# Seven block products in place of eight in two of four dense layers, and a contraction-outer loop in the other two

## The chip, the cores and the metric

The program runs on one core of one Trainium2 chip. The time is device microseconds of one execution; lower is better. A profiled execution gives the trace from which all rows below are read.

## The reference, cut to what matters

Two batches of 448 tokens, 12 heads of width 64, give 768 channels. The attention has a soft cap (tanh) ahead of the softmax. Its output goes through an RMS norm and two feed-forward blocks, all in float32:

```python
scores = cap * np.tanh(scale * (q @ k.T) / cap)          # 2 x 12 heads, 448 x 448
attn = softmax(scores); x = attn @ v                      # 896 tokens x 768
xn = x / rms(x) * rms_g
y = (silu(xn @ w_gate) * (xn @ w_val)) @ w_out            # 768 -> 2 x 1536 -> 768
h = y @ w_in; g = max(h, 0) + alpha * min(h, 0)           # 768 -> 2048
out = g @ w_out2                                          # 2048 -> 768
```

## The kernel before

**Products in three parts.** TensorE multiplies in a 32-bit format of reduced precision (`F32R`). Every float32 operand is therefore split into a rounded part and the rest (`h` and `l`, "hi" and "lo"), and a product takes three matmuls: `wh*xh`, `wh*xl`, `wl*xh`. A matmul here has a 128x128 weight tile and 448 moving columns (one batch of tokens, a "half"). `products` writes them: for each of `n_k` contraction tiles, three matmuls for each half.

**Weights.** All weights lie in one stream of 68 units of six 128x128 tiles in 64-bit floats. A unit is loaded (`w_load`, 768 KB), turned into a 32-bit float by a ScalarE cast (`w_abs`) and a VectorE operation (`w_bits`, line 96), and split by ScalarE (`w_hi`) and VectorE (`w_lo`, line 113). `step(u)` does this some units ahead, once per unit that TensorE has used up.

**Layers.** An output tile of 128 channels is made at a time, with all its contraction tiles in one PSUM bank for each half. The layer gate/value takes 24 output tiles of 6 contraction tiles, `w_out` 6 of 12, `w_in` 16 of 6 and the last 6 of 16: 864 + 432 + 576 + 576 = 2448 matmuls.

**Attention.** 48 steps (12 pairs of heads, four groups `g`): `qk`, then the ScalarE functions in `soft`, then `pv` of two steps before. Hooks put with `at(n, ...)` follow step `n`: `prep` (VectorE splits q and k of the next pair), `evac` (the PSUM results `oa`, `ob` are copied to SBUF, and a row of sums goes by DMA to `gt`), `recip` (VectorE reciprocal of the row sums of two pairs, then two GpSimd-issued DMAs that put them in `r2`, called r in the trace), `norm` (TensorE spreads `r2` over partitions into `rps`, VectorE multiplies, and squares are summed for the RMS), `rms` and `xnorm`. GpSimd computes only the squares and their sums.

**The passage from attention to the layers.** The last pairs' `recip`, `norm` and `rms` run beside `fill(m, 0)`: five half-size products that need only the first batch. Then `xnorm_last` makes the second batch's operand, `fill(m, 1)` uses it, and the main loop begins.

**Order.** Each engine runs its instructions in the order in which the program writes them (`manual_schedule`). TensorE, VectorE, ScalarE and GpSimd each have one queue; DMAs are issued from SP's queue, apart from those of `recip` and one constant (GpSimd's) and another constant (ScalarE's).

Of the kernel before, what the change touches and what calls it, by code (L numbers as in the profile page):

```python
# [17 lines left out]
P = 128  # L18
# [20 lines left out]
NFILL = 2  # L39
# [6 lines left out]
def attn_moe_kernel(ctx: ExitStack, tc: tile.TileContext, qk_in, v, sel, w, gvec, alpha, cap, out):  # L46
# [4 lines left out]
    hfill = ctx.enter_context(tc.tile_pool(name="hfill", bufs=1))  # L51
    tmp = ctx.enter_context(tc.tile_pool(name="tmp", bufs=2))
# [34 lines left out]
    def w_abs(u):
        if u < n_units and u not in top_t:
            top_t[u] = tops[u % 2]
            nc.scalar.copy(top_t[u].bitcast(F16)[:, 1::2], raw_t[u].bitcast(BF16)[:, 4:4 * UW + 4:4])  # L90

    def w_bits(u, parts=(0, 1)):
        if u < n_units and 1 in parts and u not in bits_t:
            t = wpool.tile([P, UW], U32, tag="wt", name="wt", bufs=3)
            bits_t[u] = t
            nc.vector.scalar_tensor_tensor(  # L96
                out=t, in0=raw_t[u].bitcast(U32)[:, 1:2 * UW + 1:2], scalar=13, in1=top_t[u],
                op0=ALU.logical_shift_right, op1=ALU.bitwise_or,
            )

    def w_hi(u, home=None):
        if u < n_units and u not in wh_t:
            if home is None:
                wh_t[u] = wpool.tile([P, UK, P], F32R, tag="wh", name="wh", bufs=4)
            else:
                wh_t[u], wl_t[u] = home()
            nc.scalar.copy(wh_t[u], bits_t[u].bitcast(F32).rearrange("p (k m) -> p k m", m=P))  # L107

    def w_lo(u, force=False):
        if u < n_units and (force or u not in wl_t):  # L110
            if not force:
                wl_t[u] = wpool.tile([P, UK, P], F32R, tag="wl", name="wl", bufs=4)
            nc.vector.tensor_tensor(  # L113
                out=wl_t[u], in0=bits_t[u].bitcast(F32).rearrange("p (k m) -> p k m", m=P), in1=wh_t[u],
                op=ALU.subtract,
            )
# [79 lines left out]
    ea, eb, xt, gt = {}, {}, {}, {}  # L196
# [40 lines left out]
    def norm(i):  # L237
# [3 lines left out]
        x = sb.tile([P, S], F32, tag="xt", name="xt", bufs=6)  # L241
        xt[i] = x
# [18 lines left out]
    def rms(b):  # L261
# [3 lines left out]
        rstd[b] = sb.tile([P, S], F32, tag="rstd", name="rstd", bufs=1)  # L265
# [3 lines left out]
    xh, xl = {}, {}  # L269

    def xnorm(i):
        b, p = divmod(i, NP)
        if p == 0:
            xh[b] = xpool.tile([P, KD, S], F32R, tag=f"xh{b}", name="xh")
            xl[b] = xpool.tile([P, KD, S], F32R, tag=f"xl{b}", name="xl")
        xn = sb.tile([P, S], F32, tag="xn", name="xn", bufs=1)
        nc.vector.scalar_tensor_tensor(
            out=xn, in0=xt.pop(i), scalar=g_t[:, p:p + 1], in1=rstd[b], op0=ALU.mult, op1=ALU.mult
        )
        nc.vector.tensor_copy(xh[b][:, p, :], xn)  # L280
# [20 lines left out]
    def products(dst, j0, n_k, rh, rl, halves, tail=None):


        for kx in range(n_k):
            u, o = divmod(j0 + kx, UK)
            first, last = kx == 0, kx == n_k - 1
            for hs in halves:
                nc.tensor.matmul(dst(hs), wh_t[u][:, o, :], rh(kx, hs), start=first, stop=False)  # L308
            for hs in halves:
                nc.tensor.matmul(dst(hs), wh_t[u][:, o, :], rl(kx, hs), start=False, stop=False)  # L310
            for hs in halves:
                nc.tensor.matmul(dst(hs), wl_t[u][:, o, :], rh(kx, hs), start=False, stop=last)  # L312
            if tail and o == UK - 1:
                tail(u)

    hh, hl = {}, {}
    xhf = lambda kx, hs: xh[hs][:, kx, :]
    xlf = lambda kx, hs: xl[hs][:, kx, :]

    def gate_a(sg, gp):  # L320
        nc.scalar.activation(out=sg, in_=gp, func=AF.Sigmoid)
        nc.vector.tensor_tensor(out=sg, in0=gp, in1=sg, op=ALU.mult)

    def gate_b(f, sg, vp, hsl):
        nc.vector.tensor_tensor(out=sg, in0=vp, in1=sg, op=ALU.mult)
        nc.scalar.copy(hh[f][:, hsl], sg)
        yield
        nc.vector.tensor_tensor(out=hl[f][:, hsl], in0=sg, in1=hh[f][:, hsl], op=ALU.subtract)

    def h_tiles(pool, f):  # L330
        hh[f] = pool.tile([P, 2, S], F32R, tag=f"hh{f}", name="hh")
        hl[f] = pool.tile([P, 2, S], F32R, tag=f"hl{f}", name="hl")

    def run(gen):
        for _ in gen:
            pass

    fill_ps, fill_t, sgs = {}, [None], {}

    def fill(n, half):  # L340

        f, which = divmod(n, 2)
        if half == 0 and which == 0 and f < NFILL:
            h_tiles(hfill, f)
# [307 lines left out]
```

## Time and profile before

| | |
|---|---|
| time, median of 3 runs | 630.99 us (630.76 to 631.55) |
| time of the profiled execution | 632.72 us |
| its span, first to last instruction | 630.7 us |
| TensorE busy | 617.6 us, 98% |
| VectorE busy | 299.3 us, 47% |
| ScalarE busy | 308.4 us, 49% |
| GpSimd busy | 34.3 us, 5% |
| mean granted TensorE clock | 0.997 of full |

The shares are means over the whole span. Matmuls are pipelined, so that a busy TensorE is not one at its peak: the pitch from one matmul's start to the next one's says more. The share of the other engines says little on its own, since each stage has its own mix; what ends each wait is in the rows below.

### The profile page before, as it was taken

The numbers are of one execution on the slowest core, as the hardware profiler recorded it, in microseconds if no ns is written. First come the engines' busy times: TensorE is split into PE (matmuls) and PEld (weight loads), VectorE is DVE, ScalarE is ACT, GpSimd is POOL, SyncE is SP. The second block draws the span as 40 slices with busy tenths as digits, with TensorE's granted clock in tenths as the row PEclk, the third lists the DMA queues.
The fourth block names the chain that finished last, engine by engine and source line by source line (L and its number), as shares of the span: only waits on it lengthen the run. The fifth ranks groups of instructions, "written<-read, shape, count | busy, mean of one in ns | idle before, by whom it ended". The sixth has DMA issues, their size and how long they took to land.

```text
span 630.7 us, 6973 instructions
## 1 busy us (share of the span) xinstructions
PE 617.6 (98%) x2852; PEld 538.0 (85%) x2852; DVE 299.3 (47%) x356; ACT 308.4 (49%) x368; POOL 34.3 (5%) x33
## 2 busy tenths in 40 slices
PE   5999989999999999999999999999999999999997
PEld 4666656678999999999999999999999999999996
DVE  7349766958645554444443331455555552232200
ACT  5899979934443443333332223566665652322300
POOL 0013521320000000000000000000000000000000
PEclk9999989999999999999999999999999999999999
DMA  7476464130143333322343331332333224243200
GB/s 244 158 257 223 147 221 139 29 103 0 51 150 101 101 105 125 121 101 101 106 144 120 123 109 50 101 101 100 104 122 123 103 87 150 111 162 130 79 30 29
DMA packets 19039, 73.47 MB, mean 116 GB/s; under 512 B 6080, under 2 KB 6464, under 8 KB 19008
## 3 DMA queue, kind: packets, MB, share of 16 engines
q1 hardware_dynamic: 15456, 72.81, 33.2%
q0 software_dynamic: 3408, 0.23, 0.5%
q8 instruction: 22, 0.36, 0.2%
q14 instruction: 9, 0.07, 0.0%
q10 hardware_dynamic: 144, 0.00, 0.0%
HBM read 70.14 MB, written 2.75 MB: 116 GB/s over the span
## 4 chain that ended last, share of the span: by engine, by line
PE 86%; ACT 7%; DMA 3%; DVE 2%; issue 1%; POOL 0%; DVEq 0%; POOLq 0%; ACTq 0%
PE m L308 24%; PE m L310 24%; PE m L312 24%; PE s L162 4%; PE oa L188 3%; ACT pt L173 3%; PE ob L192 2%; ACT pt L172 2%; DMA r<-tl 2%; PE fs L308 1%; PE fs L310 1%; PE fs L312 1%; DMA rw<-qk_in 1%; ACT top L90 1%; DMA gt<-eb 1%
## 5 line engine op out<-in xcount | busy, mean ns | idle before, releaser
L113 DVE TENSOR_TENSOR wl<-wt,wh 128x768 fp32r<-128x768 f32 x67 | 64.2, 958 | 105.6 <-ACT wh L107 105.5
L90 ACT CAST top<-raw 128x768 f16<-128x768 bf16 x68 | 73.0, 1073 | 29.5 <-DMA raw<-w_in 29.5
L107 ACT CAST wh<-wt 128x768 fp32r<-128x768 f32 x67 | 55.5, 828 | 35.9 <-DVE wt L96 19.9
L96 DVE SCALAR_TENSOR_TENSOR wt<-raw,top 128x768 uint32<-128x768 uint32 x68 | 64.6, 951 | 1.6 <-ACT top L90 1.6
L308 PE MATMUL m<-xh,wh 128*128 128x448 f32 x228 | 64.8, 365 | 0.0
L312 PE MATMUL m<-xh,wl 128*128 128x448 f32 x228 | 64.7, 365 | 0.0
L310 PE MATMUL m<-xl,wh 128*128 128x448 f32 x228 | 64.7, 365 | 0.0
L312 PE MATMUL m<-zh,wl 128*128 128x448 f32 x192 | 57.1, 365 | 0.0
L310 PE MATMUL m<-zl,wh 128*128 128x448 f32 x192 | 57.1, 365 | 0.0
L308 PE MATMUL m<-zh,wh 128*128 128x448 f32 x192 | 57.1, 365 | 0.0
L162 PE MATMUL s<-hi 128*128 128x448 f32 x96 | 49.7, 517 | 6.5 <-DVE hi L387 6.5
L310 PE MATMUL m<-y_xl,wh 128*128 128x448 f32 x192 | 54.5, 365 | 0.0
L308 PE MATMUL m<-y_xh,wh 128*128 128x448 f32 x192 | 54.5, 365 | 0.0
L312 PE MATMUL m<-y_xh,wl 128*128 128x448 f32 x192 | 54.5, 365 | 0.0
L172 ACT ACTIVATE pt<-s,cinv 128x896 f32<-128x896 f32 (+1 forms) x48 | 43.5, 907 | 6.7 <-PE s L162 5.2
L173 ACT ACTIVATE pt<-pt,cap_t 128x896 f32<-128x896 f32 (+1 forms) x48 | 45.6, 950 | 1.6
L310 PEld LDWEIGHTS m<-xl,wh 128*128 128x128 f32 x228 | 42.8, 188 | 3.4
L308 PEld LDWEIGHTS m<-xh,wh 128*128 128x128 f32 x228 | 42.8, 188 | 3.4
L312 PEld LDWEIGHTS m<-xh,wl 128*128 128x128 f32 x228 | 42.8, 188 | 3.4
L192 PE MATMUL ob<-pt,vt 128*128 128x448 f32 x96 | 42.0, 543 | 0.0
L310 PE MATMUL m<-hl,wh 128*128 128x448 f32 x144 | 40.9, 365 | 0.0
L308 PE MATMUL m<-hh,wh 128*128 128x448 f32 x144 | 40.9, 365 | 0.0
(122 smaller groups left out, 927.2 us busy)
## 6 DMA issues: line engine op xcount, KB each, us to landing
raw<-w_in SPq DMA_DIRECT2D x68, 768.0 KB, 4.3
rw<-qk_in SPq DMA_DIRECT2D x11, 928.0 KB, 4.9
vt<-v_in SPq DMA_DIRECT2D x12, 416.0 KB, 5.5
out<-o SPq DMA_DIRECT2D x5, 448.0 KB, 2.7
rw<-qk_in SPq DMA_DIRECT2D x1, 480.0 KB, 4.4
rw<-qk_in SPq DMA_DIRECT2D x1, 448.0 KB, 5.5
out<-o SPq DMA_DIRECT2D x2, 224.0 KB, 1.9
gt<-ea SPq DMA_DIRECT2D x12, 1.8 KB, 1.6
```

What stands on the lines that cost most here:

```text
L90: nc.scalar.copy(top_t[u].bitcast(F16)[:, 1::2], raw_t[u].bitcast(BF16)[:, 4:4 * UW + 4:4])
L96: nc.vector.scalar_tensor_tensor(out=t, in0=raw_t[u].bitcast(U32)[:, 1:2 * UW + 1:2], scalar=13, in1=top_t[u], op0=ALU.logical_shift_right ...
L107: nc.scalar.copy(wh_t[u], bits_t[u].bitcast(F32).rearrange("p (k m) -> p k m", m=P))
L113: nc.vector.tensor_tensor(out=wl_t[u], in0=bits_t[u].bitcast(F32).rearrange("p (k m) -> p k m", m=P), in1=wh_t[u], op=ALU.subtract,)
L162: nc.tensor.matmul(s[:, n, :S], hi[i][:, S + o:S + o + P], t[hd], start=(m == 0), stop=(m == len(mm) - 1),)
L172: nc.scalar.activation(out=t[:, :n], in_=s[:, :n, :S], func=AF.Tanh, scale=cinv)
L173: nc.scalar.activation(out=t[:, :n], in_=t[:, :n], func=AF.Exp, scale=cap_t)
L188: nc.tensor.matmul(oa[i][:, :S], lhs, r, start=(h == "A" and c == 0), stop=(h == "T"))
L192: nc.tensor.matmul(ob[i][:, :S], lhs, r, start=(h == "T"), stop=(h == "B" and c == 2))
L308: nc.tensor.matmul(dst(hs), wh_t[u][:, o, :], rh(kx, hs), start=first, stop=False)
L310: nc.tensor.matmul(dst(hs), wh_t[u][:, o, :], rl(kx, hs), start=False, stop=False)
L312: nc.tensor.matmul(dst(hs), wl_t[u][:, o, :], rh(kx, hs), start=False, stop=last)
```

## The change

The layers with 768 inputs (gate/value, called `g`, and `w_in`, called `z`) are cut into 2x2 blocks: the weight in output halves and contraction halves (`A11` to `A22`), the input in contraction halves and batches (`B11` to `B22`). Seven block products take the place of eight. They need sums of weight blocks (`S1` to `S4`, made on GpSimd from the 32-bit weights), differences of input blocks (`T1` to `T4`, VectorE), and sums of the products (`u2`, `u3`, `add22`, `add21`, `add12`, on VectorE; a first copy on ScalarE). Each sum and difference is split into hi and lo again.

A "slot" is one product of one unit: 18 matmuls for one group `g` of output tiles. There are 6 groups in layer `g` and 4 in layer `z`; the first two groups go side by side, the others one after another. All other work hangs on slots as hooks: `do(n, rank, fn)` puts `fn` behind the matmuls of slot `n` in program order. The four weight blocks of a group are converted by `conv` (cast and bits).

The layers `w_out` (`o`) and the last (`f`) have the contraction outside and three output tiles at a time; a slot is one unit of 36 matmuls. Their inputs are split by `ksplit`.

In the attention phase the copy of `ob` (`eb`) moves from ScalarE to VectorE, eight units are converted in place of seven, and the eight weight sums of the first two groups are made there. The diff, cut to its core:

```diff
+    def w_sum(out, a, b, op, home=None):
+        t = f_t[home] if home else f_tile()
+        nc.gpsimd.tensor_tensor(out=t, in0=f_t[a], in1=f_t[b], op=op)
+        f_t[out] = t
...
+    def sums(lay, g):
+        n = (lay, g)
+        w_sum((*n, "S1"), (*n, "A21"), (*n, "A22"), ALU.add)
+        w_sum((*n, "S3"), (*n, "A11"), (*n, "A21"), ALU.subtract, home=(*n, "A21"))
...
-            nc.scalar.copy(eb[i], ob.pop(i)[:, :S])
+            nc.vector.tensor_copy(eb[i], ob.pop(i)[:, :S])
...
+    def product(ps, u, name, first):
+        wh, wl = h_t.pop(u), l_t.pop(u)
+        xh, xl = oper[name]
+        for r in range(2):
+            mm = [(a[:, r * K3 + k, :], x[:, k, :]) for k in range(K3) for a, x in ((wh, xh), (wh, xl), (wl, xh))]
+            for n, (lhs, rhs) in enumerate(mm):
+                nc.tensor.matmul(
+                    ps[:, r, :S], lhs, rhs, start=first and n == 0, stop=n == len(mm) - 1,
...
+        for u in conv_seq[:2]:
+            at(3, w_load, u)
+        for j, u in enumerate(conv_seq[:]):
+            s0 = 7 + 5 * j
+            at(s0, w_top, u)
+            at(s0 + 1, w_bits, u)
+            if j < 6:
+                at(s0 + 1, w_next, u)
+            if u[2] in ("A11", "A12"):
+                at(s0 + 2, w_hi, u)
+                at(s0 + 3, w_lo, u)
+            if u[2] == "A22":
+                at(s0 + 2, sums, "g", u[1])
+                at(s0 + 3, sum2, "g", u[1])
+            if u[2] == "A12":
+                at(s0 + 4, sum4, "g", u[1])
...
         recip(len(members) - 1)
-        fill(0, 0)
+        product(pa[0], ("g", 0, "A11"), "B11", True)
         norm(last - 3)
         norm(last - 2)
-        fill(1, 0)
+        first_sum(0, ct("c21"))
+        product(pa[1], ("g", 1, "A11"), "B11", True)
         norm(last - 1)
         norm(last)
-        fill(2, 0)
+        first_sum(1, ct("c21"))
+        product(pa[0], ("g", 0, "A12"), "B21", False)
+        w_hi(("g", 0, "S1"))
         rms(B - 1)
...
+        product(pa[1], ("g", 1, "A12"), "B21", False)
+        w_lo(("g", 0, "S1"))
+        w_hi(("g", 1, "S1"))
+        for i in range((B - 1) * NP, (B - 1) * NP + K3):
+            xnorm(i)
...
+        def operand(name, src):
+            pool = xpool if name in ("B11", "B21", "B22") else main
+            h, l = (pool.tile([P, K3, S], F32R, tag=f"{name}{p}", name=f"x{p}") for p in "hl")
+            nc.scalar.copy(h, src)
+            tt(l, src, h, ALU.subtract)
+            oper[name] = (h, l)
+
+        def t1(b11, b12):
+            tt(b11, b12, b11, ALU.subtract)
+            operand("T1", b11)
...
+        t1(x0[:, lo3], x1[:, lo3])
+        for i in range((B - 1) * NP + K3, B * NP):
+            xnorm(i)
+        w_lo(("g", 1, "S1"))
...
+        STEADY = ("P1", "P6", "P5", "P7", "P2", "P4", "P3")
...
+        layer("g", G1, ("P5", "P6", "P7", "P4", "P3"))
...
+        layer("z", G2, ("P1", "P5", "P2", "P6", "P7", "P4", "P3"))
...
+            if n >= 2:
+                early = u[2] == "A11" and u[1] >= 2
+                do(n - 2 - early, 0, w_hi, u)
+                do(n - 2 - early, 2, w_lo, u)
...
+                for d, x in ((-6, "A11"), (-5, "A21"), (-4, "A22"), (-2, "A12")):
+                    convs.append((b + d, (lay, g, x)))
+                do(b - 4, 4, sums, lay, g)
+                do(b - 3, 4, sum2, lay, g)
+                do(b + 3, 4, sum4, lay, g)
...
+            do(at_["P6"] + 1, 1, u2_first if both else u2, g, lambda: cu("c12"))
+            do(at_["P7"] + 1, 1, u3, g, lambda: cu("c22"))
+            do(at_["P7"] + 1, 1, add22, g)
+            do(at_["P7"] + 2, 1, gate, g, 3, c22, None)
+            do(at_["P4"] + 1, 1, add21, g)
+            do(at_["P4"] + 2, 1, gate, g, 2, c21, None)
+            do(at_["P3"] + 1, 1, add12, g)
+            do(at_["P3"] + 2, 1, gate, g, 1, c12, None)
+        do(0, 0, t2, x0[:, lo3], x1[:, hi3])
+        do(1, 5, t3, x1[:, lo3], x1[:, hi3])
+        do(3, 5, t4, x0[:, hi3], x0[:, lo3])
+        do(5, 5, operand, "B22", x1[:, hi3])
...
+        do(z0, 1, lambda: operand("B21", yf[1][:, lo3]))
+        do(z0 + 2, 1, lambda: t2(yf[0][:, lo3], yf[1][:, hi3]))
+        do(z0 + 4, 5, lambda: t3(yf[0][:, hi3], yf[1][:, hi3]))
+        do(z0 + 6, 5, lambda: t4(yf[1][:, lo3], yf[0][:, lo3]))
+        do(z0 + 8, 5, lambda: operand("B22", yf[1][:, hi3]))
...
+        f0 = at_of["f", 0, 0]
+        do(f0 - 2, 5, ksplit, "f", 0, zt, ("T2h", "T2l", "T1h"), ("B11h", "B11l", "kx"))
```

## Rows read from the trace of the kernel before

**Rows 1.** Waits of TensorE: line waited for, total us, times, longest us.

```profile
PE rps L240 <- DMA r<-tl: 2.8, 2, 2.1
PE fo L310 <- DVE xl L296: 0.2, 1, 0.2
```

**Rows 2.** Timeline of TensorE: start us, us, instruction; ends are modelled, starts count.

```profile
126.36 0.71 PE L308 MATMUL fs<-xh,wh 128*128 128x448 f32 x1
...
146.00 0.37 PE L308 MATMUL fo<-xh,w_fill 128*128 128x448 f32 x1
...
148.47 0.36 PE L308 MATMUL fo<-xh,wh 128*128 128x448 f32 x1
...
339.99 0.57 PE L308 MATMUL m<-hh,wh 128*128 128x448 f32 x2
...
342.42 0.56 PE L308 MATMUL m<-hh,wh 128*128 128x448 f32 x2
```

**Rows 3.** Instruction groups by line and shape: busy us, mean ns, idle before.

```profile
L113 DVE TENSOR_TENSOR wl<-wt,wh 128x768 fp32r<-128x768 f32 x67 | 64.2, 958 | 105.6 <-ACT wh L107 105.5
L96 DVE SCALAR_TENSOR_TENSOR wt<-raw,top 128x768 uint32<-128x768 uint32 x68 | 64.6, 951 | 1.6 <-ACT top L90 1.6
...
L328 DVE TENSOR_TENSOR hl<-sg,hh 128x896 fp32r<-128x896 f32 x10 | 10.9, 1092 | 2.4 <-ACT hh L326 1.2 <-issue 0.2
...
L325 DVE TENSOR_TENSOR sg<-m,sg 128x896 f32<-128x896 f32 x10 | 10.9, 1091 | 24.6 <-PE m L312 24.6
...
L326 ACT CAST hh<-sg 128x896 fp32r<-128x896 f32 x10 | 9.5, 947 | 43.9 <-DVE sg L325 41.8 <-issue 2.1
...
L291 DVE SCALAR_TENSOR_TENSOR xn_last<-xt,g_t,rstd 128x448 f32<-128x448 f32 x6 | 4.0, 680 | 0.0
...
L328 DVE TENSOR_TENSOR hl<-sgf,hh 128x448 fp32r<-128x448 f32 x4 | 2.5, 625 | 2.5 <-ACT hh L326 2.5
```

**Rows 4.** Timeline of VectorE, late in the attention phase.

```profile
104.48 2.95 DVE L267 RECIPROCAL rstd<-rstd 128x448 f32<-128x448 f32 x1 [4.18 <-ACT rstd L266]
...
128.19 0.63 DVE L281 TENSOR_TENSOR xl<-xn,xh 128x448 fp32r<-128x448 f32 x1
```

**Rows 5.** Timeline at the end of attention, SP's queue, TensorE and VectorE; last, landing of r's DMAs.

```profile
127.47 0.50 SPq L206 DMA_DIRECT2D gt<-eb  x1
...
135.35 0.65 PE L240 MATMUL rps<-r,sel_t 128*128 128x448 f32 x2 [0.72 <-DMA r<-tl]
...
144.91 1.28 DVE L291 SCALAR_TENSOR_TENSOR xn_last<-xt,g_t,rstd 128x448 f32<-128x448 f32 x2
...
DMA to landing us min/median/max: 2.0/4.2/8.3
```

**Rows 6.** Timeline of VectorE and GpSimd where both work, and where they don't collide.

```profile
117.71 0.96 DVE L96 SCALAR_TENSOR_TENSOR wt<-raw,top 128x768 uint32<-128x768 uint32 x1
117.82 1.64 POOL L251 TENSOR_TENSOR sq<-xt 128x448 f32<-128x448 f32 x1 [5.33 <-DVE xt L244]
...
118.59 1.35 DVE L277 SCALAR_TENSOR_TENSOR xn<-xt,g_t,rstd 128x448 f32<-128x448 f32 x1
...
119.54 1.41 POOL L255 TENSOR_TENSOR s<-s,sq 128x448 f32<-128x448 f32 x1
...
119.98 1.23 DVE L280 CAST xh<-xn 128x448 fp32r<-128x448 f32 x1
...
123.41 0.39 DVE L280 CAST xh<-xn 128x448 fp32r<-128x448 f32 x1
...
137.85 0.62 DVE L244 TENSOR_TENSOR xt<-eb,rps 64x448 f32<-64x448 f32 x1
137.93 1.15 POOL L255 TENSOR_TENSOR s<-s,sq 128x448 f32<-128x448 f32 x1 [2.12 <-ACT sq L253]
```

**Rows 7.** Stretches of TensorE: length, busy us, granted clock, DMA share, GB/s.

```profile
83.60:85.70 2.10, 0.00 (x0) 1.00 0.53 193
85.70:89.20 3.50, 3.49 (x10) 0.51 0.46 141
```

More of the change, by code (lines that the diff above doesn't have):

```diff
@@ L87, in w_abs @@
[L87 to L116, printed above, removed]
+        raw_t[u] = wpool.tile([P, 4 * UW + 4], U16, tag="raw", name="raw", bufs=2)
@@ L194, in pv @@
             del q2[i], hi[i], vt[i]
-    ea, eb, xt, gt = {}, {}, {}, {}
+    ea, eb, gt = {}, {}, {}
+    xf = [xpool.tile([P, KD, S], F32, tag=f"b{b + 1}", name="xf") for b in range(B)]
     group = {}
@@ L301, in products @@
[L301 to L344, printed above, removed]
-        if (f, half) not in ((NFILL, 0), (0, 1)):
-            if which == 0:
-                fill_t[0] = ps_s.tile([P, 2, 512], F32, tag="s", name="fs")
-            t = fill_t[0][:, which, :S]
-        else:
-            t = ps_o.tile([P, 512], F32, tag="o", name="fo")[:, :S]
-        fill_ps[f, half] = fill_ps.get((f, half), ()) + (t,)
-        products(lambda hs: t, n * UK, KD, xhf, xlf, [half])
@@ L571, in attn_moe_kernel @@
[L571 to L588 removed]
+            return pair_tile(*pools[(turn[0] - 1) % 4])
@@ new lines, in attn_moe_kernel, with layer @@
+        STEADY = ("P1", "P6", "P5", "P7", "P2", "P4", "P3")
+        def layer(lay, n_g, start):
+            for p in start:
+                for g in range(2):
+                    pslot(lay, p, g)
+            for g in range(2, n_g):
+                for p in STEADY:
+                    pslot(lay, p, g)
+        hb, zt = {}, {}
+        layer("g", G1, ("P5", "P6", "P7", "P4", "P3"))
+        for half in range(2):
+            for u in range(K1 // 2):
+                oslot("o", half, u, K1 // 2, lambda kk, l: 2 * kk + l)
@@ new lines, in attn_moe_kernel, with h_of @@
+        for g in range(2):
+            do(z0 - 2, 4, sums, "z", g)
+            do(z0 - 1 + g, 4, sum2, "z", g)
+            do(z0 + 3 + g, 4, sum4, "z", g)
+        convs.sort(key=lambda c: c[0])
+        for n, u in convs:
+            conv_seq.append(u)
+            do(n, 3, conv, u)
+        for u in conv_seq[6:8]:
+            do(0, 6, w_next, u)
+        def h_of(g):
+            if g % 2 == 0 and g // 2 not in hb:
+                hb[g // 2] = block(g // 2)
+            return hb[g // 2][:, g % 2 * 4:g % 2 * 4 + 4, :]
@@ new lines, in attn_moe_kernel, with u2_first @@
+        twelve = {}
+        def u2_first(g, _):
+            if g == 0:
+                twelve[0] = block(3)
+            u2(g, lambda: twelve[0][:, 2 * g:2 * g + 2, :])
+        for g in range(G1):
+            at_ = {p: at_of.get(("g", g, p)) for p in STEADY}
+            both = g < 2
+            if not both:
+                do(at_["P1"] + 1, 1, lambda g: first_sum(g, ct("c21")), g)
+            do(at_["P2"] + 1 if not both else g, 1, gate, g, 0, pa, (lambda: cu("c11")) if both else (lambda: ct("c11")))
+            do(at_["P6"] + 1, 1, u2_first if both else u2, g, lambda: cu("c12"))
[6 more added lines that the diff above has]
+            do(at_["P3"] + 2, 1, gate, g, 1, c12, None)
@@ new lines, in attn_moe_kernel, with y_put @@
+        o0 = at_of["o", 0, 0]
+        do(o0 - 2, 5, ksplit, "o", 0, hb, ("T2h", "T2l", "T3h"), 3)
+        do(o0 - 1, 5, ksplit, "o", 1, hb, ("T3l", "B21h", "B21l"), 0)
+        do(o0 + 2, 5, ksplit, "o", 2, hb, ("T4h", "T4l", "B22h"), 1)
+        yf = {}
+        def y_put(half):
+            yf[half] = block(2 + half)
+            for m in range(3):
+                nc.scalar.copy(yf[half][:, m:m + 4:3, :], banks[m][:, :, :S])
+        y0 = at_of["o", 1, 0]
+        do(y0 - 1, 9, y_put, 0)
+        do(y0 + 1, 5, lambda: operand("B11", yf[0][:, lo3]))
```

399 lines of the change are left out of this document (239 added, 160 removed).

## The prediction

> **What bounds the kernel now.** I read first the waits of TensorE: behind its start it waits 3.0 us in all, for the row sums at the end of a pair of heads and for one split [rows 1]. Then the timeline of its matmuls. In the main loop twelve starts take 342.42 - 339.99 = 2.43 us, 0.2025 us for each, without a gap [rows 2]. The five half-size fills run from 126.36 to 148.47 us: 22.1 us for 90 matmuls worth 18.2, so that the whole passage from attention into the layers costs 3.9 us [rows 2]. TensorE bounds everything behind 126 us, and VectorE's 47% hides there. A matmul less is therefore worth 0.2025 us, as long as the other queues keep up.
>
> **What is removed.** Each group of output tiles takes seven slots of 18 matmuls in place of eight, with ten groups: 180 matmuls fewer, 2268 for 2448. That is 180 x 0.2025 = **-36.5 us**. A slot lasts 18 x 0.2025 = 3.65 us. The product's order (nine matmuls in a row into one bank, one half) is that of the fills; from 146.00 to 148.47 us those took 0.206 a matmul [rows 2]. On the 1260 matmuls of the new slots that is 0 to 4.2 us; the timeline has no slot of the new kind in the main pools, and I take half, **+2.1**.
>
> **Prices.** VectorE: a split or bit operation of 768 columns 0.96 and 0.95 us, an operation of 896 columns 1.09 whether its input lies in PSUM or SBUF, of 448 columns 0.62, the normalization 0.68 [rows 3]. The step from 448 to 896 gives 1.56 for the 1344 columns of an input block. ScalarE: 0.95 for 896, in proportion 0.81 for 768 and 1.42 for 1344. A difference T takes VectorE, then a ScalarE copy that VectorE's queue waits for, then VectorE: 1.56 + 1.42 + 1.56 = 4.55. Each VectorE operation starts some 0.03 us behind the last.
>
> GpSimd's weight sums are not in the trace. A sum of 448 columns takes 1.15 us [rows 6], in proportion 1.97 for 768; there are 40. What do they cost VectorE? From 117.71 to 121.21 us three VectorE operations that alone take 0.95, 0.68 and 0.39 [rows 3, 6] needed 3.50 us beside two GpSimd operations: 1.48 us lost, 0.74 for each, 1.27 in proportion for 768. VectorE's multiplication from PSUM at 137.85 took its usual 0.62 beside a sum [rows 6]. About a third of VectorE's work in the layers reads PSUM (6.1 of the 18.5 us of a group, below), so a sum costs VectorE between 0 and 1.97 us; I take **0.9** there and 1.27 in the attention phase, nearest the collision seen.
>
> [...]
>
> **The start.** VectorE works without a pause from 104.48 to 128.82 us [rows 4], since the reciprocal stands in its queue until ScalarE delivers. Before, that delayed nobody: ScalarE evacuated the last `ob`, and its DMA left at 127.47 [rows 5]. Now that copy stands behind this stretch, which also gets four `eb` copies (0.6 each), one more bit operation, one more split, and two S4 sums at 1.27: +6.9 us, to 135.7. The row-sum DMA, `recip`, r's DMA and the spreading into `rps` follow; they took 127.47 to 135.35 us [rows 5]. Two weight loads flew then and don't now; r's landings go from 2.0 to 4.2 and 8.3 us, and I take 1.5 off. The spread comes at 135.7 + 7.9 - 1.5 = 142.1.
>
> TensorE has by then run its two products and idled for over 5 us. After an idle of 2.1 us the trace shows 3.5 us at a granted clock of 0.51, the level of 1.2 GHz, worth 1.75 us [rows 7]; it now falls on the third product, ahead of the RMS sums. From the spread to the reciprocal's end took 144.91 - 135.35 = 9.56. Then VectorE does a split, three normalizations and T1 (0.96 + 2.1 + 4.55, with gaps 7.8). The first slot starts at 142.1 + 9.56 + 1.75 + 7.8 = 161.2. With 72 matmuls (14.6) done since 126.36, that loses 20.3 us where the old passage lost 3.9: **+16.4**.
>
> **The head of layer g.** Between T1 and the third group's first slot VectorE has, in its order: 3 normalizations 2.1, ten splits 9.6, T2 to T4 13.7, B22's lo 1.6, five gate products 3.1, nine product sums 9.8, four bit operations 3.8; 43.7, with gaps 1.0 and three GpSimd sums at 0.9, **47.4 us**. The slot needs the bank that `add12` of group 0, the last of these, frees. TensorE's ten slots take 36.5. The loss is **+10.9**, of which the waits fall on `u2` and `u3` (P7 and P4 add into the bank that these read) and on that bank. A second fall of the clock lies inside this loss, since TensorE has to wait anyway.
>
> **Layer g further on** has 18.5 us of VectorE work (seven splits 6.7, four bit operations 3.8, five product sums 5.5, four gate products 2.5) and 3.6 for GpSimd's sums against 25.5 of TensorE's seven slots: nothing, and TensorE's matmuls are the cover. At the entry of `o` a bank waits for `add21` behind `ksplit`: +0.3.
>
> **The head of layer z.** B21's lo can end 4.8 us into it (the last output copy, a split and B21's copy on ScalarE, 0.95 + 0.81 + 1.42, then 1.56). Then thirteen splits 12.5, T2 to T4 13.7, B22 1.6, four bit operations 3.8, nine sums 9.8, five prelu operations 5.5: 46.9, gaps 1.2, six GpSimd sums 5.4; together 58.3 against 14 slots, 51.0: **+7.3**. Groups 2 and 3 hold 20.4 + 3.6 against 25.5: nothing. At the entry of `f` the third bank waits for `add21`, which stands behind two prelu operations and a `ksplit` of 4.2 us: 11.7 us after the slot P4 began, against 7.3 + 2.4 on TensorE: **+2.0**.
>
> **The rest.** The contraction-outer loops have the same matmuls, and their splits are spread over 87 and 117 us with VectorE about a third busy: nothing, and at most the 2.4 us of twelve matmuls at each change of halves if the copies were late. The last output tile is now copied and sent in two parts behind the last matmul, +0.5. ScalarE gives up twelve copies of 448 columns in attention, some 6 us; its gain is between 0 and 6, and since TensorE is the fuller engine there I take -1.
>
> **Sum.** -36.5 + 2.1 + 16.4 + 10.9 + 0.3 + 7.3 + 2.0 + 0.5 - 1.0 = +2.0 us. The profiled execution took 632.7 us (span 630.7, 2 around it) and lies 1.7 above the median; on the median of 631.0 the forecast is **633 us**, with 626 to 640 as its own range: the seven products save what they promise, and VectorE's queue gives it back in three places. About 0.2% (1.3 us) is what a measurement of this kernel can tell from no change.
>
> **Rivals.**
>
> *GpSimd's sums cost VectorE nothing* (they fall beside its PSUM work or its pauses). Then 2.5 + 2.7 + 5.4 = 10.6 us go: 622. For it: the overlap at 137.85 [rows 6]; against it: the lost 1.48 us.
>
> *VectorE clears its backlog before attention ends*, say because ScalarE, relieved, delivers `rstd` early. VectorE's pause ahead of the reciprocal was 4.2 us [rows 4]. If the last copy left at 127.5 as before, TensorE would not idle ahead of the spread, and 8 us and the clock's 1.75 go: 623. Both of these together give 613.
>
> *VectorE becomes the bound throughout, slower.* One sum costs VectorE its full 1.97: then a steady group of `g` takes 18.5 + 7.9 = 26.4 against 25.5 and one of `z` 28.3, which is +3.6 over four groups and +5.6 over two; the two heads get 9 x 1.07 more and attention's two sums 1.4: +20.2, 653. It decides from about 1.75 us a sum, where 18.5 + 7.0 fill the group; for it speaks VectorE's cast of 0.39 us that took 1.23 beside a sum, against it the total of 1.48 us over two [rows 6]. [...]
>
> *TensorE doesn't gain what the count says*: a pitch of 0.206 in every new slot, another +2.1; it moves the sum and decides nothing.
>
> **How the numbers follow.** The forecast gets 0.45, the two faster rivals 0.35 together, the slower one 0.20. The low end is both faster rivals, 615 (a rest of 0.1 below), the high end 648, near the full price of the sums (0.1 above). Faster by over 0.2%: 0.33 of the faster rivals and 0.12 of the forecast's own spread, 0.45. Same: 0.10 and 0.02, 0.12. Slower: 0.23 and 0.20, 0.43.
>
> **What the profile of the changed kernel would show.** 2268 matmuls behind attention's own, at 0.2025 to 0.206. TensorE waiting for r's DMA once for 5 to 8 us and then for T1's lo for 7 to 8 us, with a granted clock near 0.5 behind each. The last `eb` copy on VectorE at about 136 us. VectorE over 90% busy in the ten first slots of `g` and in the first 14 of `z`, with TensorE's waits named `u2`, `u3`, `add12`. GpSimd's sums at 1.8 to 2.9 us. No wait of TensorE inside `o` and `f`. The prediction is wrong if VectorE has pauses in the two heads, if TensorE's first slot starts before 155 us, or if the steady groups take more than 26 us.

## The result, and the profile after

The changed kernel takes 633.84 us (median of 20 runs, 630.9 to 638.0) against 630.72 beside it; ratio 1.0059 [1.0042, 1.0076], slower by more than a measurement can miss. Its profiled execution took 631.3 us, one of its shortest, with a span of 629.5. Before's profiled execution (632.72 us, mean clock 0.997, with the low clock of [rows 7]) lies 2.0 above its median and is of a rarer kind: of 63 later runs 8 took 633.4 to 633.7 at a mean granted clock of 0.996 or 0.997, the others at most 631.3 at 0.999 or 1.000.

The page of the changed kernel, engines and the two groups that answer to [rows 3] and to the sums (columns as there):

```profile
PE 592.0 (94%) x2672; PEld 506.9 (81%) x2672; DVE 424.6 (67%) x442; ACT 349.2 (55%) x418; POOL 117.2 (19%) x73
...
L124 DVE TENSOR_TENSOR wl<-wt,wh 128x768 fp32r<-128x768 f32 x98 | 108.3, 1114 | 71.0 <-ACT wh L120 70.9
L115 POOL TENSOR_TENSOR wt<-wt 128x768 f32<-128x768 f32 x40 | 84.2, 2108 | 279.6 <-DVE wt L107 167.6
```

TensorE is busy 592.0 us in place of 617.6: it gives up work and idles instead. The longest waits of TensorE behind its start answer to [rows 1], which hold 3.0 us (line waited for, total us, times, longest):

```profile
PE m L338 <- ACT xh L494: 5.6, 1, 5.6
PE s L338 <- DVE b L488: 4.8, 4, 2.4
PE s L201 <- ACT pt L211: 4.6, 2, 2.8
PE m L338 <- DVE b L488: 4.0, 3, 2.0
PE s L201 <- DVE q L181: 1.6, 1, 1.6
PE s L338 <- DVE b L739: 1.5, 1, 1.5
PE m L564 <- DVE b L488: 1.2, 1, 1.2
PE s L566 <- DVE ks L488: 1.0, 1, 1.0
```

Line 488 is VectorE's helper: `b` stands for the product sums, `xl` and `xh` (line 494, ScalarE) for T1. Nearly all waits end at VectorE's queue or a copy that it holds up. Two were not foreseen, both in attention: `q` of line 181 (at 82.9 us, where VectorE's two splits took 4.28 us, in place of 2 x 0.62, beside GpSimd's first sums) and, larger, `pt` of line 211, the tanh. ScalarE's timeline late in attention shows where the second comes from:

```profile
108.89 0.83 ACT L120 CAST wh<-wt 128x768 fp32r<-128x768 f32 x1 [3.14 <-DVE wt L107]
109.63 1.00 ACT L211 ACTIVATE pt<-s,cinv 128x896 f32<-128x896 f32 x1
...
125.68 0.83 ACT L120 CAST wh<-wt 128x768 fp32r<-128x768 f32 x1 [4.27 <-DVE wt L107]
126.42 1.00 ACT L211 ACTIVATE pt<-s,cinv 128x896 f32<-128x896 f32 x1
```

ScalarE's queue stands 3.14 and 4.27 us at the cast `w_hi` of an A12 unit, because VectorE, busy 23.7 of the 24.3 us from 104.48 to 128.82, is late with that unit's bits; the next tanh stands behind the cast, and TensorE behind the tanh. So the first layer product starts at 134.51 us, where the first fill started at 126.36 before [rows 2]. A matmul of attention that stands at the same place in both programs, the 305th, starts at

```profile
98.65 0.71 PE L162 MATMUL s<-hi 128*128 128x448 f32 x1
```

before and in the changed kernel at

```profile
96.38 0.71 PE L201 MATMUL s<-hi 128*128 128x448 f32 x1
```

The changed kernel is 2.3 us ahead there, since it has the 1.6 us for `q` where before has 2.1 and the low clock of [rows 7]. From there to the first product it loses 10.4 us: 134.51 - 96.38 = 38.1 in place of 126.36 - 98.65 = 27.7.

TensorE's timeline at the passage, around VectorE's reciprocal, last `eb` copy and T1:

```profile
134.51 0.71 PE L338 MATMUL s<-xh,wh 128*128 128x448 f32 x1
...
143.41 0.65 PE L281 MATMUL rps<-r,sel_t 128*128 128x448 f32 x2 [0.63 <-DMA r<-tl]
...
158.49 0.74 PE L338 MATMUL m<-xh,wh 128*128 128x448 f32 x1 [5.58 <-ACT xh L494]
160.14 0.74 PE L338 MATMUL m<-xl,wh 128*128 128x448 f32 x1 [0.91 <-DVE xl L488]
...
204.38 0.44 PE L338 MATMUL m<-xh,wh 128*128 128x448 f32 x1 [1.31 <-DVE b L488]
```

```profile
135.06 0.62 DVE L261 COPY eb<-ob 128x448 f32<-128x448 f32 x1 [0.78 <-PE ob L231]
...
149.91 2.95 DVE L307 RECIPROCAL rstd<-rstd 128x448 f32<-128x448 f32 x1 [3.49 <-ACT rstd L306]
...
158.52 1.56 DVE L488 TENSOR_TENSOR xl<-xf,xh 128x1344 fp32r<-128x1344 f32 x1 [1.48 <-ACT xh L494]
```

The last copy comes at 135.06 (forecast 135.7), the spread at 143.41 (142.1), T1's lo lets the second matmul go at 160.14 (161.2), and the third group's first slot starts at 204.38. Behind five of the waits the granted clock is at the lower of its two levels for a while, as in [rows 7]; behind others, such as that of 1.61 us which ends at 426.84, it stays at 1.00. Stretches of the changed kernel, with the columns that the windows view names:

```profile
core 0: us, PE busy (x) PEld busy (x) DVE busy (x) ACT busy (x) POOL busy (x), PEclk, DMA share, GB/s
150.00:160.00 10.00, 3.65 (x16) 2.59 (x14) 8.49 (x8) 2.65 (x3) 0.00 (x0) 0.82 0.00 1
160.00:170.00 10.00, 9.86 (x42) 8.99 (x43) 8.31 (x11) 4.31 (x5) 0.00 (x0) 0.84 0.00 0
180.00:190.00 10.00, 7.60 (x31) 6.65 (x30) 9.62 (x10) 7.03 (x9) 0.00 (x0) 0.83 0.29 88
424.00:432.00 8.00, 6.39 (x32) 5.54 (x31) 7.87 (x8) 6.25 (x8) 0.00 (x0) 1.00 0.10 15
450.00:460.00 10.00, 7.34 (x28) 6.24 (x28) 6.92 (x7) 8.24 (x12) 0.19 (x1) 0.83 0.23 80
```

### The profile page after: what moved, and what is told of

It is laid out like the page before. It is cut to its first block, busy times and chain, and to the rows that moved or that the text cites. A ratio compares the mean times of both kernels' runs of the same rounds, so it can differ in the third digit from the quotient of the medians.

```text
span 629.5 us, 6931 instructions
## 1 busy us (share of the span) xinstructions
PE 592.0 (94%) x2672; PEld 506.9 (81%) x2672; DVE 424.6 (67%) x442; ACT 349.2 (55%) x418; POOL 117.2 (19%) x73
## 4 chain that ended last, share of the span: by engine, by line
PE 68%; DVE 18%; ACT 5%; issue 5%; DMA 2%; POOL 1%; ACTq 0%; DVEq 0%; POOLq 0%
PE m L338 12%; PE s L338 11%; PE s L568 6%; PE s L564 6%; PE s L566 6%; PE m L564 5%; PE m L568 5%; PE m L566 5%; PE s L201 5%; PE oa L227 4%; DVE wl L124 4%; PE ob L231 4%; DVE b L488 3%; DVE wt L107 1%; ACT zn L738 1%
## 5 line engine op out<-in xcount | busy, mean ns | idle before, releaser
L124 DVE TENSOR_TENSOR wl<-wt,wh 128x768 fp32r<-128x768 f32 x98 | 108.3, 1114 | 71.0 <-ACT wh L120 70.9
L115 POOL TENSOR_TENSOR wt<-wt 128x768 f32<-128x768 f32 x40 | 84.2, 2108 | 279.6 <-DVE wt L107 167.6
L338 PE MATMUL s<-xh,wh 128*128 128x448 f32 x228 | 85.1, 373 | 6.2 <-DVE b L488 4.8
L338 PE MATMUL s<-xh,wl 128*128 128x448 f32 x228 | 84.0, 369 | 0.0
L338 PE MATMUL s<-xl,wh 128*128 128x448 f32 x228 | 84.0, 368 | 0.0
L338 PEld LDWEIGHTS s<-xh,wh 128*128 128x128 f32 x228 | 43.3, 190 | 11.8 <-ACT wh L120 3.3
L564 PE MATMUL s<-ks,wh 128*128 128x448 f32 x176 | 50.0, 365 | 0.0
L568 PE MATMUL s<-ks,wl 128*128 128x448 f32 x176 | 50.0, 365 | 0.0
L564 PE MATMUL m<-ks,wh 128*128 128x448 f32 x160 | 45.5, 366 | 1.2 <-DVE b L488 1.2
L568 PE MATMUL m<-ks,wl 128*128 128x448 f32 x160 | 45.4, 365 | 0.0
```

Source lines behind the costliest of these rows:

```text
L115: nc.gpsimd.tensor_tensor(out=t, in0=f_t[a], in1=f_t[b], op=op)
L124: nc.vector.tensor_tensor(out=l_t[u], in0=f_t[u].rearrange("p (k m) -> p k m", m=P), in1=h_t[u], op=ALU.subtract)
L338: nc.tensor.matmul(ps[:, r, :S], lhs, rhs, start=first and n == 0, stop=n == len(mm) - 1, skip_group_check=True,)
L564: nc.tensor.matmul(dst[l], wh[:, o, :], xh[l], start=first, stop=False)
L568: nc.tensor.matmul(dst[l], wl[:, o, :], xh[l], start=False, stop=fin)
```

## The experiments

**What do GpSimd's sums cost?** The first run leaves them out:

```diff
-        t = f_t[home] if home else f_tile()
-        nc.gpsimd.tensor_tensor(out=t, in0=f_t[a], in1=f_t[b], op=op)
-        f_t[out] = t
+        f_t[out] = f_t[home or a]
```

> Leaves out all 40 of GpSimd's weight sums (S1 to S4 are then just one of the blocks they are made from), so that the outputs are not the reference's. Theory (VectorE's queue gives the gain back, a sum costs it about 0.9 us): VectorE's busy time falls from 424.6 by some 36 us, the waits of TensorE for product sums at the heads shrink by 3 us each, attention ends some 4 us earlier; the time falls from 633.8 by 9 to 13 us, to about 622. If the two engines blocked each other for the whole instruction, VectorE's busy time would fall by some 80 us (40 x 2.1). Rival (VectorE's own operations are the load, the sums lie in its pauses): the time stays above 630.

Measured: 625.34 us (622.63 to 631.36), 8.5 under the changed kernel (9 to 13 expected), ratio to before 0.9925 [0.9901, 0.995]. The page, engines and the same group as above (now line 122):

```profile
PE 589.3 (95%) x2672; PEld 507.0 (82%) x2672; DVE 384.3 (62%) x442; ACT 349.4 (56%) x418; POOL 33.0 (5%) x33
...
L122 DVE TENSOR_TENSOR wl<-wt,wh 128x768 fp32r<-128x768 f32 x98 | 92.3, 951 | 70.4 <-ACT wh L118 70.3
```

VectorE's 442 operations take 384.3 us in place of 424.6, and a split is back at 0.95, near the 0.96 of [rows 3]. On average one sum costs VectorE 40.3 / 40 = 1.01 us, for a duration of 2.11; that is a tenth above the 0.9 taken, and both rivals on this price fall, nothing and the full duration. The rows by operation and shape tell who pays, with the sums

```profile
L488 DVE TENSOR_TENSOR b<-c 128x448 f32<-128x448 f32 x16 | 15.0, 936 | 0.0
...
L488 DVE TENSOR_TENSOR c<-m,c 128x896 f32<-128x896 f32 x12 | 13.1, 1089 | 5.2 <-PE m L338 5.1
```

and without:

```profile
L486 DVE TENSOR_TENSOR c<-m,c 128x896 f32<-128x896 f32 x12 | 13.1, 1091 | 8.5 <-PE m L336 8.4
...
L486 DVE TENSOR_TENSOR b<-c 128x448 f32<-128x448 f32 x16 | 9.9, 618 | 0.0
```

The forms that get longer read two operands in SBUF: the splits take 16.0 us more in all, the bit operations 8.6, `b<-c` 5.1, seven others the rest. Those with one input in PSUM (`m`, `s`) take the same beside a sum and without one. The Trainium skill ("SBUF — State Buffer", section "Who interferes with whom") says that a VectorE instruction with two SBUF inputs contends with a GpSimd instruction that reads SBUF; the trace agrees, and the half is the mean over operations that pay and operations that don't. By stage the run gains 2.1 us up to T1, 1.7 in the head of g and 4.2 in z, of 2.5, 2.7 and 5.4 worked out; it doesn't part VectorE's price from waits for a sum itself.

**Is ScalarE's stand in attention the loss?** One run moves the splits of the two A12 units and their S4 sums: group 0's go five steps later, group 1's behind the attention steps. The other only gives the `eb` copy back to ScalarE:

```diff
-            if u[2] in ("A11", "A12"):
-                at(s0 + 2, w_hi, u)
-                at(s0 + 3, w_lo, u)
+            if u[2] in ("A11", "A12") and j < 7:
+                late = 5 if j == 6 else 0
+                at(s0 + 2 + late, w_hi, u)
+                at(s0 + 3 + late, w_lo, u)
...
-            if u[2] == "A12":
-                at(s0 + 4, sum4, "g", u[1])
+            if u[2] == "A12" and j < 7:
+                at(s0 + 9, sum4, "g", u[1])
...
+        w_hi(("g", 1, "A12"))
+        w_lo(("g", 1, "A12"))
...
         rms(B - 1)
+        sum4("g", 1)
```

> The split of the two A12 units moves from inside the last attention steps to behind them. Theory (new here: in attention ScalarE's queue stands behind that split, which waits for VectorE's late bit operation, and so the tanh that TensorE needs is late): ScalarE's waits of 3.1 and 4.3 us for the bits vanish, with TensorE's waits of 1.8 and 2.8 us and the low clock behind them; attention ends near 128 us in place of 134.5; but the last eb copy still stands behind VectorE's other work, so that T1 comes only 2 to 4 us earlier: 630 to 632. Rival (TensorE's late end of attention is what makes T1 late): 7 us less, 627.

```diff
-            nc.vector.tensor_copy(eb[i], ob.pop(i)[:, :S])
+            nc.scalar.copy(eb[i], ob.pop(i)[:, :S])
```

> The copy of ob goes back to ScalarE, as before the change. Theory: VectorE's stretch at the end of attention loses four copies of 0.6 us, its bit operations come earlier, so ScalarE's waits for them shrink by 1 to 2 us each; the time falls by 2 to 4 us, to 630 to 632. Rival (ScalarE is the fuller engine in attention, and the copies were better on VectorE): the first 90 us take longer by 2 us or more, and the time is 634 or above.

Measured: 631.56 us (629.66 to 635.94; ratio to before 1.0026 [1.0007, 1.0046]) and 631.91 (630.12 to 635.7; 1.003 [1.0013, 1.0048]), 2.3 and 1.9 under the changed kernel. In the first, TensorE's timeline shows the loss move rather than go:

```profile
141.41 1.08 PE L281 MATMUL rps<-r,sel_t 128*128 128x448 f32 x2 [5.88 <-DMA r<-tl]
...
159.87 0.74 PE L338 MATMUL m<-xl,wh 128*128 128x448 f32 x1 [0.91 <-DVE xl L492]
```

Attention ends earlier (the first product starts at 127.26), and now TensorE waits 5.88 us for r's DMA, which is the wait that had been forecast; T1 comes 0.3 us earlier, where 2 to 4 were expected. (With the casts, VectorE's splits of these units and GpSimd's sums move too, so that this run does not remove ScalarE's stand by itself.) Giving the copy back alone brings T1's second matmul to 159.53, 0.6 us earlier.

> The changed kernel with the last A12 conversions and sum behind attention and the last eb copy on ScalarE, without the chunks and the moved splits: the two edits that took 631.6 and 631.9 alone. If they only add, -2.3 and -1.9: 629 to 630. Theory (each alone leaves the row sums' copy late by the other engine's queue; both are needed, and then the first slot comes 6 to 8 us earlier, as between the last two of the runs before): 626 to 628, with the second matmul behind T1 starting at 152 to 154 us.

Both edits together: 628.71 us (625.42 to 631.32), ratio 0.9962 [0.9942, 0.9983]. That lies between the two times expected; the timeline decides. In TensorE's, the spread and T1 are

```profile
134.24 0.66 PE L281 MATMUL rps<-r,sel_t 128*128 128x448 f32 x2 [0.85 <-DMA r<-tl]
...
153.31 0.74 PE L338 MATMUL m<-xl,wh 128*128 128x448 f32 x1 [0.91 <-DVE xl L492]
```

6.8 us earlier than in the changed kernel, where the edits alone brought 0.3 and 0.6. Two queues held the same chain: ScalarE's delayed the last scores, VectorE's the copy of the row sums. (This profiled execution, like that of the late splits, ran the later groups of g and layer o at the slow pitch told below: 104.2 and 89.3 us for 102.2 and 87.6. Without these 3.7 us its 628.21 would be 624.5, which is 6.8 under the changed kernel's 631.3. The late splits alone come to 631.0 in this way, and the copy alone took 630.6, so that the traces give these two 0.3 and 0.7 of the 2.3 and 1.9 at the medians.)

**Are T and the operands long chains?** Each difference and split is cut into three parts of 448 columns, so that a copy and a split start as soon as their part is there:

```diff
-            nc.scalar.copy(h, src)
-            tt(l, src, h, ALU.subtract)
+            for j in range(K3):
+                nc.scalar.copy(h[:, j], src[:, j])
+            for j in range(K3):
+                tt(l[:, j], src[:, j], h[:, j], ALU.subtract)
...
+        def diff(out, a, b):
+            for j in range(K3):
+                tt(out[:, j], a[:, j], b[:, j], ALU.subtract)
...
-            tt(b11, b12, b11, ALU.subtract)
+            diff(b11, b12, b11)
```

> The differences T and the splits of input blocks are made in three parts of 448 columns each, so that VectorE goes on while ScalarE copies. Theory (in the heads VectorE's queue is full, with 1.4 us in each T spent on waiting for ScalarE's copy): these waits vanish, T1 is ready 1.5 to 2.5 us earlier, each head is shorter by 2 to 3 us; the time falls by 5 to 8 us, to 626 to 629. Rival (the waits don't matter, since three short operations cost VectorE as much more as the wait took): 632 to 635.

Measured: 625.53 us (625.4 to 628.76), ratio 0.9934 [0.9918, 0.995]: the same work (VectorE is busy 424.3 us in place of 424.6), and faster than both kernels. From the spread to T1's second matmul it takes 158.03 - 143.72 = 14.3 us in place of 16.7; from there to the third group's first slot 200.47 - 158.03 = 42.4 in place of 44.2; layer z takes 499.94 - 390.24 = 109.7 in place of 111.6. That makes 6.1 us; the profiled executions are 5.9 apart, and the rest of the 8.3 between the medians lies in how the runs spread.

**Does layer z pay?** Layer z by eight products again, g by seven:

```diff
-        layer("z", G2, ("P1", "P5", "P2", "P6", "P7", "P4", "P3"))
+        for g in range(G2):
+            zslot(g, "A11", "B11", "T1", True)
+            zslot(g, "A12", "B21", "B22", False)
+            zslot(g, "A21", "B11", "T1", True)
+            zslot(g, "A22", "B21", "B22", False)
```

Here `zslot` runs one unit's 36 matmuls, against both batches' blocks (B11 and B12, which is called T1 here, or B21 and B22); the sums and differences of z go.

> Layer z goes back to eight block products (four slots of 36 matmuls per group, no weight sums, no differences T, no product sums in z); layer g keeps its seven. Theory (z's seven products save 4 x 18 = 72 matmuls, 14.6 us, and VectorE's queue gives back the waits at z's head, 7.1 us in the changed kernel's trace, 1.4 us of low clock and some of the 2.5 us at the entry of f): +14.6 - 7.1 - 1.4 - 1 to 2 = +4 to +5, so 637 to 640 beside 633.8 (the profiled execution 635 to 637 beside 631.3). Rival (z's seven products gain nothing, all of it is given back): 633 to 634. Rival (the waits at z's head come from layer g's end and stay): +14.6 = 648.

Measured: 637.88 us (634.33 to 642.22), ratio 1.0102 [1.0059, 1.0145], 4.0 above the changed kernel. From z's first matmul to f's first it takes 518.01 - 398.98 = 119.0 us in place of 505.78 - 394.16 = 111.6, without a wait of TensorE, and f's entry loses nothing. The 119.0 are at a slow pitch of 0.2067 (at the usual one 576 matmuls make 116.6), so that z's seven products keep some 3 of their 14.6 us. At the usual pitch that is 116.6 - 111.1 - 2.5 = 3.0, where 111.1 is 111.6 without its 0.5 of slow pitch and 2.5 is lost at f's entry; with both at the slow pitch (2.0 more for 504 matmuls) it is 119.0 - 113.1 - 2.5 = 3.4. The medians say 4.0, but their intervals touch; it is the traces that carry this.

**More order.** On top of the parts, both splits of both S1 units go ahead of the reciprocal, and f's first split one slot forward:

```diff
-        w_hi(("g", 0, "S1"))
+        for g in range(2):
+            w_hi(("g", g, "S1"))
+            w_lo(("g", g, "S1"))
         rms(B - 1)
...
-        w_lo(("g", 0, "S1"))
-        w_hi(("g", 1, "S1"))
...
-        w_lo(("g", 1, "S1"))
...
-        do(f0 - 2, 5, ksplit, "f", 0, zt, ("T2h", "T2l", "T1h"), ("B11h", "B11l", "kx"))
+        do(f0 - 3, 5, ksplit, "f", 0, zt, ("T2h", "T2l", "T1h"), ("B11h", "B11l", "kx"))
```

> The differences and operands in parts of 448 columns, as in the run before that took 625.5; besides, both splits of both S1 sums stand ahead of the reciprocal of the RMS, where VectorE and ScalarE pause, and the first split of f's input goes one slot earlier. Theory (VectorE's order behind the reciprocal sets T1 and the third group's first slot): one split, 0.95 us, and its wait for ScalarE leave the stretch ahead of T1 and the two slots of f's entry lose 1.2 to 2.5 us less: 621 to 624. Rival (the stretch ahead of T1 is set by something other than that split, f's entry by the banks): 625 to 626, no change against the chunks alone.

Measured: 623.94 us (623.27 to 626.78), ratio 0.989 [0.9862, 0.9917], 1.6 under the parts alone. The two waits at f's entry are gone (2.5 us), and from T1 to the third group 41.6 us are left; but from the spread to T1 it still takes 159.97 - 145.31 = 14.7. Moving the splits did not shorten that.

**All together**: the run above, with late A12 conversions and the copy on ScalarE.

> The run with chunks and order, and besides the last A12 conversions of group 1 and its S4 sum behind the attention steps and the last eb copy on ScalarE again. Theory (ScalarE's tanh no longer stands behind a cast that waits for VectorE, so attention ends some 4 to 6 us earlier, and the row sums leave earlier, since neither engine's queue holds their copy up): both halves are needed together, as each alone left the first slot where it was (159.87 and 159.53 against 160.14); together the first slot comes 4 to 8 us earlier: 614 to 619. Rival (the chain of the row sums' transfers and the RMS sets T1 whatever the two queues do): 620 to 624, as the run without these two edits.

Measured: 617.88 us (615.8 to 623.76), ratio 0.9796 [0.9755, 0.9836]. T1's second matmul starts at 152.04, 8.1 us before the changed kernel's; TensorE's longest waits behind its start are

```profile
PE m L338 <- DVE b L492: 5.6, 3, 2.2
PE m L338 <- ACT xh L499: 4.6, 1, 4.6
```

**Why do the runs spread?** The changed kernel's 20 runs lie within 7.1 us, those of before beside them within 1.6. In the traces the products' matmuls run at one of two pitches, 0.2027 or 0.2067 us. A first guess was the order, nine in a row into one bank:

```diff
-        for r in range(2):
-            mm = [(a[:, r * K3 + k, :], x[:, k, :]) for k in range(K3) for a, x in ((wh, xh), (wh, xl), (wl, xh))]
-            for n, (lhs, rhs) in enumerate(mm):
+        mm = [(a, k, x[:, k, :]) for k in range(K3) for a, x in ((wh, xh), (wh, xl), (wl, xh))]
+        for n, (a, k, rhs) in enumerate(mm):
+            for r in range(2):
```

> The changed kernel, only the order of a product's 18 matmuls is different: each weight part goes to the first and then to the second tile of the contraction, so that the two banks alternate, where nine in a row went to one bank. The same work. The traces so far show that matmuls of the seven products run at either 0.2027 or 0.2067 us from start to start, for a whole stretch between two waits, and differently in each execution; those of the two other layers always at 0.2025. Theory (nine in a row into one bank with a moving operand that changes allow the slow pitch; the alternation does not): all stretches at 0.2025 to 0.203, median 630 to 632 beside 633.8, highest run under 633. Rival (something else picks the pitch): both pitches still there, median 633 to 634.5, runs up to 637.

> The run with everything together (617.9 median, 615.8 to 623.8) with the same new order of a product's matmuls. Theory (the slow pitch is what spreads its runs): 615 to 616.5, highest under 618. Rival: 617 to 619 with runs over 620.

Measured: 633.23 us (630.76 to 637.0; ratio 1.0042 [1.0021, 1.0063]) and 619.13 (615.13 to 622.66; 0.9803 [0.9762, 0.9843]). The guess is wrong: the spread stays, and in the first one layer f, whose order was not touched, ran at the slow pitch from 511 us to its end. Then both kernels once more, nothing edited:

> The changed kernel once more, nothing edited, for a second profiled execution. Its first took 631.3 us, with 120 of some 1200 recorded matmuls of the seven products at a pitch of 0.2067 us and the rest at 0.2027; its other runs took 630.9 to 638.0. Theory (the pitch is picked anew in each execution and makes most of the spread between runs): the profiled time is 631.3 + 0.004 x (slow matmuls - 120), within 1 us, so 631 to 636. Rival (the pitch is a matter of the program, the spread lies elsewhere, in the attention phase or the transfers): the same stretches are slow as in the first profile, whatever the time.

> The kernel with everything together once more, nothing edited. Its first profiled execution took 615.9 us with 83 of some 1220 recorded matmuls at 0.2067; its other runs 615.8 to 623.8. Theory: 615.9 + 0.004 x (slow matmuls - 83), within 1 us, so 615.6 to 620.5; a time above 620.5 is more than the pitch can explain. Rival: the same stretches are slow as in the first profile, whatever the time.

Measured: 635.45 and 615.39 us. Two steady stretches of the changed kernel (in layer g; in layer o), in its first profile

```profile
210.00:230.00 20.00, 20.00 (x101) 18.53 (x100) 17.36 (x16) 9.39 (x13) 7.98 (x4) 1.00 0.45 146
...
330.00:350.00 20.00, 20.00 (x101) 18.54 (x100) 2.99 (x4) 3.74 (x5) 0.00 (x0) 1.00 0.34 119
```

and in its second:

```profile
210.00:230.00 20.00, 20.00 (x99) 18.16 (x98) 17.15 (x16) 10.10 (x13) 7.98 (x4) 1.00 0.41 135
...
330.00:350.00 20.00, 20.00 (x99) 18.16 (x98) 5.41 (x6) 4.55 (x5) 0.00 (x0) 1.00 0.35 119
```

The same program, full clock, no wait, and 2% fewer matmuls. From the third group's first slot to z's first wait are 1044 matmuls (504 in g, 432 in o, 108 in z). TensorE's timeline of both gives the ends, in the first

```profile
417.67 0.47 PE L338 MATMUL s<-xh,wh 128*128 128x448 f32 x1 [1.46 <-DVE b L739]
```

and in the second:

```profile
204.84 0.44 PE L338 MATMUL m<-xh,wh 128*128 128x448 f32 x1 [1.51 <-DVE b L488]
...
421.86 0.47 PE L338 MATMUL s<-xh,wh 128*128 128x448 f32 x1 [1.03 <-DVE b L739]
```

Without their last gaps (1.63 and 1.20 us) that is 211.7 and 215.8 us, 0.2027 and 0.2067 each; the difference of 4.1 is the whole difference of the two spans, 629.5 and 633.7. So the same program can run at either pitch, as the theory said, but the size was undercounted: the expectation counted the seven products alone and gave a time of about 633.7, and layer o runs slow as well. The second profile of the kernel with everything together has few slow matmuls and a short time. Over all thirteen profiles of the changed kernel and its variants, g from the third group on takes 102.1 to 102.2 or 104.2 us and o 87.6 or 89.3, both at the same level each time: nine are fast, four slow. With some 2,200 matmuls behind T1 the pitch can explain at most 8.8 us, which could cover the spread of every kernel here; how much of the spread it is was seen in one pair of profiles alone. The long stretches mostly change pitch at a wait of TensorE, and before, with 3.0 us of waits, shows no long slow stretch; but with alternating banks in the last kernel the pitch turns slow at about 404 us, 7 us ahead of the next wait. What picks the pitch stays open.

## Why the prediction was right, and where it was off

The forecast was 633 us, the median is 633.84; the seven products save what they promise, and VectorE's queue gives it back in the three places named. What the forecast did not have is the way in which the first of the three is paid. By its terms, from the two profiled executions:

| term | forecast | measured |
|---|---|---|
| 180 matmuls fewer, with the new slots' pitch | -36.5 + 2.1 | -36.5 + 0.8 |
| start, to T1's second matmul at 160.14 | +16.4 | +15.3 |
| head of g, T1 to the third group | +10.9 | +7.8 |
| steady groups of g, entry of o | +0.3 | 0 |
| z, all of it | +7.3 | +9.1 |
| entry of f | +2.0 | +2.5 |
| tail | +0.5 | +0.6 |
| ScalarE's relief | -1.0 | not seen |
| sum | +2.0 | -0.4 (spans: -1.2) |

The spans are 0.8 below the sum because before's own matmuls behind its fills take 1.0 us more than 0.2025 each, which no term holds. That the medians say +3.1 is no contradiction: before's profiled execution lies 2.0 us above its median, which no term holds either, and the changed kernel's 2.5 below its own. So that 633 came within a microsecond is in part luck. The head of g was 3.1 us too high and the start 1.1, while z was 1.8, f's entry 0.5 and the pitch 1.2 too low, if the 2.5 at the median are all pitch.

- **The saving** is real: steady groups run without a gap, at 0.2027. The pitch term was right in kind, "0 to 4.2 us", but its two ends are two levels, and which one holds is drawn per stretch. The profiled execution drew mostly the fast one (0.5 us of slow pitch); at the median the changed kernel takes 2.5 us more, which the slow level could pay.
- **The start** has about the forecast size, but the step that TensorE would idle over 5 us ahead of the spread did not occur there: it waited 0.6 us for r's DMA. The stand came earlier, in attention, from ScalarE's queue behind VectorE's late bits: 10.4 us that the forecast had at nothing, with 7.1 left for the passage (160.14 - 134.51 = 25.6 us, less 14.6 of work and the 3.9 of before) and 2.3 gained on before's wait of [rows 7]. The forecast had let VectorE run full to 128 us and charged only its own copies; it had not asked who waits for the bits. Removing that stand, without the other edit, brought the forecast wait of 5.9 us back and T1 only 0.3 us forward, and both edits together removed 6.8 us. So VectorE's queue set the row sums, as argued, and would have held T1 by itself; that ScalarE's stand was no longer, and so cost nothing on top, is luck. The rival "backlog clears" priced this at 8 us and 1.75 of clock, where the two edits brought 6.8, and its 613 for both rivals counts attention's sums (2.5) twice.
- **The head of g** was oversized by 3 us. The forecast had let each VectorE operation start 0.03 us behind the last; in VectorE's timeline of the changed kernel the operations overlap instead:

```profile
199.23 0.94 DVE L124 TENSOR_TENSOR wl<-wt,wh 128x768 fp32r<-128x768 f32 x1
200.10 0.61 DVE L488 TENSOR_TENSOR b<-c 128x448 f32<-128x448 f32 x1
200.63 1.08 DVE L488 TENSOR_TENSOR c<-s,c 128x896 f32<-128x896 f32 x1
201.64 1.60 DVE L107 SCALAR_TENSOR_TENSOR wt<-raw,top 128x768 uint32<-128x768 uint32 x1
```

  a split of 0.94 is followed after 0.87, a sum of 1.08 after 1.01; over 40 operations that is an estimated 4 us with the gaps not taken. No run parts it from the other errors of this term. The last of the rows, 1.60 for 0.95 beside a GpSimd sum, is the collision.
- **Layer z** takes 111.6 us where 504 matmuls at 0.2025 make 102.1; without 0.5 of slow pitch that is a loss of 9.1: 7.1 us of gaps from one matmul's start to the next, as forecast 7.3, and some 2 us of low clock and slow first steps behind them, which the forecast had counted only for the start (granted clock 0.83 from 450 to 460 us).
- **The sums** cost 1.01 us of VectorE each. Leaving them out brought 8.5 us, near the 10.6 worked out for the heads and attention. The argument that work on PSUM is spared held in the rows of that run.
- Of the signs named, VectorE was not over 90% busy through all of g's first slots (8.31 of 10 us from 160 to 170), and f's entry had waits where none was named inside f, though the sum held 2.0 us for them. VectorE does have pauses in the heads, one of the three signs that would make the prediction wrong: from T1 to the third group it is busy 39.7 of 44.2 us. Of the missing 4.5, 4.2 are three waits of 1.39 for ScalarE's copy inside T2 to T4, which the forecast had counted in the price of a T; the sign was worded too sharply. The steady groups take 102.2 / 4 = 25.6 us, under the 26 named.

## What to carry to other kernels

Fewer matmuls paid here only where the engine that makes their operands had pauses; count its queue stage by stage, at the entry of each layer above all, and ask of each late result which *other* engine's queue stands behind it. When a chain passes two queues, an edit to one may show nothing until the other is mended too. Cutting a chain that goes from one engine to another and back (difference, copy, split) into parts cost no busy time and brought 8.3 us here, and the changes of order, with one copy given back to ScalarE, 7.7 more: together they took the same arithmetic from 633.8 to 617.9 us, 2.0% under the kernel before.

## What the runs showed of the hardware, unexpected

- TensorE's steady pitch for 128x448 matmuls has two levels, 0.2027 and 0.2067 us, at a granted clock of 1.00; the same program got the one in its first profile and the other in its second, and the two were 4 us apart for this alone.
- Back-to-back VectorE operations overlap by 0.07 us in the trace (0.94 us, followed after 0.87), so that a queue of many short ones is shorter than the sum of their durations.
- A GpSimd sum of two 768-column inputs took 2.11 us and cost VectorE 1.01 us, all of it in operations with two operands in SBUF: one of 0.62 us went to 0.94 on average, one of 1.09 that reads PSUM stayed at 1.09.
